# Reordering the first batch of a fused attention and mixer kernel: loads of pair 2, second mask, casts, second-layer weights, and a cleared mask table

## The chip, the cores and the metric

One core of one Trainium2 chip. The metric is the device time of one execution in microseconds (us), the median of several executions. The engines are named PE (matmul), ACT (scalar), DVE (vector), GpSimd (POOL in the profile) and SyncE (SP in the profile, which here only issues transfers).

## The reference, cut to what matters

Attention over 4 batches, 8 heads, 768 positions, head size 64, with a block mask (blocks of 32: neighbours, first and last blocks, three sampled blocks per row), then a mixer:

```python
scores = where(mask, q @ k.T / 8, -1e9);  attn = softmax(scores);  x = attn @ v
u  = x + (x.T @ U @ V).T                       # low rank, over positions
out = u + relu(u @ w_ch1) @ w_ch2              # 512 -> 2048 -> 512
```

The result is float32 of shape 4x768x512. The kernel works on pairs of heads: 16 pairs, 4 in each batch. Pair 0 to pair 3 are batch 0, the first batch.

## The kernel before: the parts that matter

In the first batch the mask is put into the scores by the matmul itself: the lower or upper 64 rows of `qa` and `ka` hold mask rows and one-hot rows. There are two sets of `qa` and `ka`, used by even and odd pairs; the mask rows of set 1 are a copy of those of set 0. The four queue heads at the start, with the table `small` first on ACT's queue:

```python
keep(nc.scalar.dma_start(out=small[0:NB], in_=small_dr.ap()))      # NB = 24 rows
keep(nc.sync.dma_start(out=qld[:, :, 0:TQ], in_=q0[:, :, 0:TQ]))
keep(nc.scalar.dma_start(out=kld[:, :, 0:TK], in_=k0[:, :, 0:TK])) # k's first piece
keep(nc.sync.dma_start(out=qld[:, :, TQ:T], in_=q0[:, :, TQ:T]))
keep(nc.scalar.dma_start(out=id16, in_=eye16_dr.ap()))
keep(nc.sync.dma_start(out=kld[:, :, TK:T], in_=k0[:, :, TK:T]))
...                                       # (cut)
vld = new_ld(0, "v")                      # v waits on purpose for k's first piece
keep(nc.gpsimd.tensor_copy(out=vld[:, 0, 0, 0:1], in_=kld[:, 0, 0, 0:1]))
keep(nc.sync.dma_start(out=vld, in_=src_of("v", 0)))
issue(1)                                  # pair 1's q, k, v on SyncE's queue
```

Every pair has nine units. A unit is: scores on PE, one exp of 128x1024 on ACT, values of the unit three back on PE, then what `at_unit` adds. Program order is kept on each engine:

```python
for i in range(HP):                       # HP = 4 pairs
    for u in range(NU):                   # NU = 9 units
        scores(i, u, ests[u])             # matmuls, then exp on ACT
        ...                               # (cut) values of an earlier unit
        at_unit(i, u)

def at_unit(i, u):
    if i == 0 and u == 0:                 # (cut to the part that is changed)
        for h in range(2):
            mask_rows("dve", h, pm2[:, 0, 0:QB], QA, S)
            nc.sync.dma_start(out=qa[1][h][mrows[h], :], in_=qa[0][h][mrows[h], :])
            hot_rows(nc.sync, 1, h, D)    # one-hot rows into ka[1]
        ...                               # V twice, U, then pair 2's q and k
        cast(1, "q"); cast(1, "k"); cast(1, "v")      # float32 to float16 on GpSimd
    ...
    if u == 6: cast(i + 2, "q"); cast(i + 2, "k")
    if u == 8: cast(i + 2, "v")
    for _ in range({0: 1, 5: 2, 6: 1, 7: 1}.get(u, 0)):
        if tails: tails.popleft()()       # mixer of the pair before: its xh and uh casts are on GpSimd
```

From the second batch on, scores, values and the two layers of the mixer are interleaved on PE by a fixed schedule.

The softmax here doesn't subtract the row's maximum and nothing guards it: scores larger than these inputs give would overflow.

## Time and profile before

| | before |
|---|---|
| median (3 runs at first; 283.31 to 283.8) | 283.8 us |
| span of the profiled run | 281.8 us |
| first exp starts | 7.26 us |
| first 37 exps (batch 0 and one more) end | 45.44 us |
| idle between these exps | 2.51 us |
| PE's unbroken mixer stream starts (22 matmuls `pt`) | 50.77 us |

Windows by stage of the kernel before. Columns: stretch, its length, busy time (and instructions) of PE, PE's weight loads, DVE, ACT, GpSimd, then PE's granted clock, the mean busy share of the 16 DMA engines, and GB/s.

```profile
52.00:60.00 8.00, 8.00 (x100) 4.34 (x98) 6.63 (x12) 7.43 (x12) 0.00 (x0) 1.00 2.65 125
...
80.00:120.00 40.00, 39.85 (x596) 23.63 (x594) 33.42 (x50) 29.49 (x32) 23.34 (x27) 1.00 1.27 124
```

From 52 us on PE is busy almost without a break (39.85 of each 40 us from 80 to 200 us, 19.58 of the 20 before that). A start that is earlier or later by some amount moves what is behind it by that amount (the mixer stream starts at 50.77 us here and at 51.98 in the changed kernel, and DVE's last addition ends 227.89 and 227.92 us later). So the first batch decides, and there ACT's exps are the longest work. The timeline of ACT, kernel before; columns are start, length, engine and line, operation, tiles and shapes, count, and in brackets the idle time before and what ended it.

```profile
4.66 0.40 ACT L362 CAST kst<-kld 128x256 f16<-128x256 f32 x1 [0.27 <-DMA kld<-in_k_dram]
...
7.26 6.90 ACT L494 ACTIVATE est<-psc 128x1024 f16<-128x1024 f32 x7 [0.54 <-PE psc L174]
14.49 4.69 ACT L494 ACTIVATE est<-psc 128x1024 f16<-128x1024 f32 x5 [0.33 <-PE psc L174]
19.47 3.97 ACT L494 ACTIVATE est<-psc 128x1024 f16<-128x1024 f32 x4 [0.29 <-PE psc L174]
23.95 2.94 ACT L494 ACTIVATE est<-psc 128x1024 f16<-128x1024 f32 x3 [0.51 <-PE psc L174]
28.26 17.18 ACT L494 ACTIVATE est<-psc 128x1024 f16<-128x1024 f32 x18 [1.38 <-PE psc L174]
46.28 1.94 ACT L494 ACTIVATE est<-psc 128x1024 f16<-128x1024 f32 x2 [0.84 <-PE psc L174]
```

Read it so: 18 exps in 17.18 us is ACT's own pace, 0.95 us each. Where a row ends and a new one begins, ACT had to wait for scores: 0.33, 0.29, 0.51 and 1.38 us. The last row is the step into the second batch, 0.84 us idle. The chain of waits of the kernel before, ahead of the largest gap (start, length, what):

```profile
15.62 6.63 DMA vld<-in_v_dram
...
25.07 0.83 POOL kst L248
25.91 0.45 POOL uh L655
26.35 0.47 POOL w1t L434
26.83 0.52 POOL uh L655
...
27.39 0.34 PE puT L707 x3
...
28.26 0.80 ACT est L494
```

The casts of `uh` (the mixer's float16 input for the transposes `puT`) stand on GpSimd behind pair 3's k cast, with a weight-load issue between them, and all this behind a late load of v; PE's transposes `puT` wait for uh, and the scores stand behind the transposes. SyncE's queue in the same kernel:

```profile
7.10 0.54 SPq L991 DMA_DIRECT2D qa<-qa  x1
...
8.38 0.53 SPq L991 DMA_DIRECT2D qa<-qa  x1
...
9.60 1.07 SPq L1000 DMA_DIRECT2D w2t<-in_moe_V_dram  x2
...
14.46 0.38 SPq L233 DMA_DIRECT2D qld<-in_q_dram  x1
```

Pair 2's q is issued at 14.46 us, behind the mask copies, V and U.

### The profile page before, as it was taken

Reading aid. Unit: us, or ns where it says so; the run is one execution under the profiler, and the core shown is the slowest. Engines: PE = TensorE matmul, PEld = TensorE weight load, DVE = VectorE, ACT = ScalarE, POOL = GpSimd, SP = SyncE. Lnnn points to the kernel's source line nnn. Section 1 sums busy time; section 2 is a strip of 40 time slices with the busy share of each in tenths; the row PEclk is TensorE's granted clock in tenths of the full one; section 3 lists DMA queues with packets and bytes.
Section 4 is the critical chain, followed back from the end, with each engine's and each line's share of the span. In section 5 each row is a group of like instructions: output and inputs, shape, how many; then the busy total and the mean of one; then the engine's idle time right before and its main releaser. Section 6 shows DMA issues by size and latency. Waiting matters only on the chain.

```text
span 281.8 us, 8050 instructions
## 1 busy us (share of the span) xinstructions
PE 272.5 (97%) x3497; PEld 162.3 (58%) x3497; DVE 175.1 (62%) x285; ACT 177.5 (63%) x199; POOL 100.5 (36%) x132
## 2 busy tenths in 40 slices
PE   8997998999999999999999999999999999999995
PEld 3565775456566564656665555657565544655443
DVE  6765767797888878765967767784979541000112
ACT  4997997696969847595876657596868101654000
POOL 2379857205356646361614545361102020000000
PEclk9999999999999999999999999999999999999999
DMA  5989999993979999997794999993100313000112
GB/s 173 268 240 333 238 247 187 155 117 25 95 75 112 155 122 148 139 131 83 49 123 28 142 100 134 167 111 55 30 2 2 102 22 128 31 1 2 74 74 77
DMA packets 85716, 31.71 MB, mean 112 GB/s; under 512 B 75304, under 2 KB 83312, under 8 KB 85680
## 3 DMA queue, kind: packets, MB, share of 16 engines
q0 software_dynamic: 49728, 10.10, 47.7%
q1 hardware_dynamic: 35464, 20.85, 35.0%
q8 instruction: 27, 0.44, 0.6%
q10 hardware_dynamic: 488, 0.24, 0.3%
q14 instruction: 9, 0.07, 0.1%
HBM read 27.90 MB, written 6.29 MB: 121 GB/s over the span
## 4 chain that ended last, share of the span: by engine, by line
PE 79%; DMA 6%; ACT 6%; POOL 3%; issue 2%; DVE 1%; SPq 1%; ACTq 0%; POOLq 0%; DVEq 0%
PE pt L174 29%; PE pch L174 28%; PE pav L174 10%; PE psc L174 8%; ACT est L494 6%; DMA vld<-in_v_dram 5%; PE pa L174 2%; DMA kld<-in_k_dram 1%; POOL xh L594 1%; PE ph L174 1%; POOL uh L655 1%; POOL vt L242 1%; POOL w1t L434 0%; SPq L233 0%; DVE xh L537 0%
## 5 line engine op out<-in xcount | busy, mean ns | idle before, releaser
L494 ACT ACTIVATE est<-psc 128x1024 f16<-128x1024 f32 x144 | 142.5, 1028 | 42.0 <-PE psc L174 40.4
L174 PE MATMUL pt<-uT,w1t 64*128 64x384 f16 (+1 forms) x896 | 94.6, 324 | 0.5 <-ACT est L494 0.4
L174 PE MATMUL pch<-w2t,tT 64*128 64x512 f16 (+3 forms) x688 | 93.3, 372 | 0.2
L515 DVE TENSOR_TENSOR est<-est,m 128x1024 f16<-128x1024 f16 x108 | 78.7, 745 | 17.2 <-ACT est L494 16.0
L174 PEld LDWEIGHTS <-w1t 64*128 64x128 f16 (+1 forms) x896 | 46.7, 94 | 36.5 <-PE pt L174 6.7
L174 PEld LDWEIGHTS <-tT 64*128 64x128 f16 (+1 forms) x688 | 37.7, 95 | 38.5 <-PE pch L174 1.4
L732 ACT ACTIVATE tT<-pt 128x768 f16<-128x768 f32 (+1 forms) x48 | 36.8, 776 | 33.7 <-PE pt L174 33.7
L174 PEld LDWEIGHTS <-est 128*128 128x128 f16 x1152 | 41.4, 97 | 10.9 <-issue 5.1
L174 PE MATMUL pav<-vt,est 128*128 128x65 f16 x1152 | 44.4, 193 | 0.1
L594 POOL CAST xh<-xs 128x768 f16<-128x768 f32 x12 | 11.5, 955 | 86.5 <-DVE xs L585 55.9
L787 DVE TENSOR_TENSOR of<-xf,pch 128x1024 f32<-128x1024 f32 (+3 forms) x16 | 15.3, 954 | 43.5 <-PE pch L174 43.4
L174 PE MATMUL psc<-qT,kT 64*128 64x512 f16 (+1 forms) x288 | 40.8, 323 | 0.0
L680 POOL CAST uh<-xf 128x768 f16<-128x768 f32 x12 | 13.0, 1087 | 25.2 <-issue 12.9
L174 PE MATMUL psc<-qa,ka 128*128 128x512 f16 (+1 forms) x96 | 21.5, 326 | 0.3
L734 DVE TENSOR_SCALAR tT<-pt 128x768 f16<-128x768 f32 (+1 forms) x20 | 18.2, 916 | 4.6 <-PE pt L174 4.5
L174 PEld LDWEIGHTS <-kT 64*128 64x128 f16 x288 | 14.4, 94 | 11.0 <-DVE xs L585 0.2
L262 POOL DMA_DIRECT2D qst<-in_q_dram x20 | 16.3, 821 | 0.1
L262 POOL DMA_DIRECT2D vt<-in_v_dram x20 | 16.3, 822 | 0.0
L262 POOL DMA_DIRECT2D kst<-in_k_dram x20 | 16.3, 821 | 0.0
L583 DVE RECIPROCAL rcp<-pav 128x12 f32<-128x12 f32 x12 | 2.8, 233 | 16.0 <-PE pav L174 16.0
L585 DVE TENSOR_TENSOR xs<-pav,rcp 128x768 f32<-128x768 f32 x12 | 11.5, 958 | 1.2
L671 DVE TENSOR_TENSOR xf<-xs,ph 128x768 f32<-128x768 f32 x12 | 11.4, 950 | 1.3 <-PE ph L174 1.1
(68 smaller groups left out, 134.8 us busy)
## 6 DMA issues: line engine op xcount, KB each, us to landing
out_dram<-of SPq DMA_DIRECT2D x9, 512.0 KB, 3.7
vld<-in_v_dram SPq DMA_DIRECT2D x6, 384.0 KB, 8.0
w1t<-in_moe_w_ch_dram POOLq DMA_DIRECT2D x4, 512.0 KB, 10.7
w2t<-in_moe_w_ch_dram POOLq DMA_DIRECT2D x4, 512.0 KB, 18.4
qld<-in_q_dram SPq DMA_DIRECT2D x5, 384.0 KB, 6.2
kld<-in_k_dram SPq DMA_DIRECT2D x5, 384.0 KB, 7.2
qst<-in_q_dram POOLq DMA_DIRECT2D x20, 96.0 KB, 3.9
kst<-in_k_dram POOLq DMA_DIRECT2D x20, 96.0 KB, 4.8
```

Source lines behind the costliest of these rows:

```text
L174: ins = nc.tensor.matmul(out, lhsT, rhs, start=start, stop=stop, skip_group_check=loose)
L242: nc.gpsimd.tensor_copy(out=vts[b % 2][:, 2 * hp : 2 * hp + 2, :, 0:D], in_=ld)
L262: keep(nc.gpsimd.dma_start(out=o[:, h], in_=src_of(nm, i)[:, h]))
L494: keep(nc.scalar.activation(out=est, in_=psc, func=AF.Exp, scale=0.125))
L515: keep(nc.vector.tensor_tensor(out=o, in0=o, in1=m, op=ALU.mult))
L585: nc.vector.tensor_tensor(out=xs.rearrange("p (c j) (h d) -> p c (j h) d", c=2, h=2), in0=pv[:, :, :, 0:D], in1=rcp[:, :, :, None].broadca ...
L594: keep(nc.gpsimd.tensor_copy(out=xh, in_=xs))
L671: nc.vector.tensor_tensor(out=u.rearrange("p (c j) n -> p c j n", c=2), in0=xs.rearrange("p (c j) n -> p c j n", c=2), in1=ph[:, :, 0:HS]. ...
L680: keep(nc.gpsimd.tensor_copy(out=uh, in_=u))
L732: keep(nc.scalar.activation(out=o, in_=i, func=AF.Relu))
L734: keep(nc.vector.tensor_scalar_max(out=o, in0=i, scalar1=0.0))
L787: nc.vector.tensor_add(out=of, in0=xfs[b][:, sc : sc + nsc, n0:n1], in1=pch)
```

## The change

The intent, as I read it from the diff: get pair 2's loads out early, by taking the second mask's four transfers from SyncE's queue to GpSimd's; put the casts that PE waits for ahead of those for loads to come; load the second layer's weights only in the second batch; and run the mask matmuls on all 128 rows, for which the rest of the table has to be cleared first. (The third pair is pair 2 here, as pairs count from 0.)

```diff
+    keep(nc.gpsimd.memset(small, 0.0))
     keep(nc.scalar.dma_start(out=small[0:NB], in_=small_dr.ap()))
...
-            cbd[0:NB].rearrange("z a c -> z (a c)"),      # mask matmuls
-            small[0:NB, a:e],
+            cbd.rearrange("z a c -> z (a c)"),
+            small[:, a:e],
...
-    for vt in vts:                                        # moved to the start
-        keep(nc.gpsimd.memset(vt[:, :, :, D : D + 1], 1.0))
+    for h in range(2):
+        hot_rows(nc.gpsimd, 1, h, D)
     cast(0, "v")
...
-            ((1, 3), (1, 5), (1, 7), (2, 0), (2, 3), (2, 5), (2, 7), (3, 0))
+            ((1, 3), (1, 4), (2, 3), (2, 4), (HP, 0), (HP, 2), (HP, 4), (HP, 6))
...                                                        # at_unit(0, 0)
-                    keep(nc.sync.dma_start(out=qa[1][h][mrows[h], :], in_=qa[0][h][mrows[h], :]))
-                    hot_rows(nc.sync, 1, h, D)
-                V twice, U, issue(2, "qk")
+                issue(2, "q"), U, issue(2, "k"), V twice
                 cast(1, "q")
+                for h in range(2):
+                    keep(nc.gpsimd.dma_start(out=qa[1][h][mrows[h], :], in_=qa[0][h][mrows[h], :]))
                 cast(1, "k")
...
             if u == 6:
+                cast(2, "q")
                 cast_U()
-                cast(2, "q")
...
-        at = u - 2 if i == 1 else u - 1                   # turns of the next pair
-        if at in range(4): ...
-        if u == 6: cast(i + 2, "q"), cast(i + 2, "k")
-        if u == 8: cast(i + 2, "v")
+        if u in (1, 2, 3, 4): ...
         ... tails ...
+        if u == 7: cast(i + 2, "q")
+        if u == 8: cast(i + 2, "k")
+        if u == 0 and i > 1: cast(i + 1, "v")
```

(Cut: the hook that issues the weight loads in the second batch, and the v cast of pair 5 there. Lines of several statements are drawn together.)

More of the change, by code (lines that the diff above doesn't have):

```diff
@@ L314 @@
     keep(nc.scalar.activation(out=dummy, in_=zeros[:, 0:1], func=AF.Exp))
+    for vt in vts:
+        keep(nc.gpsimd.memset(vt[:, :, :, D : D + 1], 1.0))
     vld = new_ld(0, "v")
@@ L989, in at_unit @@
                     mask_rows("dve", h, pm2[:, 0, 0:QB], QA, S)
-                    keep(
-                        nc.sync.dma_start(
-                            out=qa[1][h][mrows[h], :], in_=qa[0][h][mrows[h], :]
-                        )
-                    )
-                    hot_rows(nc.sync, 1, h, D)
                 for nm, o, pt, t in (("q", qa[0], pq, TQ), ("k", ka[0], pk, TK)):
@@ L998, in at_unit @@
                         half_copy(nc.vector.tensor_copy, o, h, pt, t, T)
-                for h in range(2):
-                    keep(nc.sync.dma_start(out=mvld[h * R : h * R + R], in_=moe_V))
+                issue(2, "q")
                 keep(
@@ L1005, in at_unit @@
                 )
-                issue(2, "qk")
+                issue(2, "k")
+                for h in range(2):
+                    keep(nc.sync.dma_start(out=mvld[h * R : h * R + R], in_=moe_V))
                 cast(1, "q")
+                for h in range(2):
+                    keep(
+                        nc.gpsimd.dma_start(
+                            out=qa[1][h][mrows[h], :], in_=qa[0][h][mrows[h], :]
+                        )
+                    )
                 cast(1, "k")
@@ L1034, in at_unit @@
             WLOADS[i, u]()
-        at = u - 2 if i == 1 else u - 1
-        if at in range(4):
-            turn_part(i + 1, "qk"[at // 2], at % 2)
-        if u == 6:
-            cast(i + 2, "q")
-            cast(i + 2, "k")
-        if u == 8:
-            cast(i + 2, "v")
+        if u in (1, 2, 3, 4):
+            turn_part(i + 1, "qk"[(u - 1) // 2], (u - 1) % 2)
         for _ in range({0: 1, 5: 2, 6: 1, 7: 1}.get(u, 0)):
@@ L1045, in at_unit @@
                 tails.popleft()()
+        if u == 7:
+            cast(i + 2, "q")
+        if u == 8:
+            cast(i + 2, "k")
+        if u == 0 and i > 1:
+            cast(i + 1, "v")
     for i in range(HP):
@@ L1069, in unit_sides @@
             turn_dma(i + 1, "k")
+        if (i, u) in WLOADS:
+            WLOADS[i, u]()
         if u in (3, 5, 7):
@@ L1104 @@
             flush_value()
+            cast(HP + 1, "v")
         if gi == 1:
```

## The prediction

> **What bounds the kernel now.** From about 48 us to the end PE is busy without a break (windows by stage: 39.85 of each 40 us), clock 1.00. The change adds nothing to that part (same instruction counts on PE, ACT, DVE; order differs only in the first batch). Time can only come from the first 48 us, the attention of batch 0, where the chain of waits runs over ACT. ACT does 36 exps of 128x1024 there, about 0.95 us each in an unbroken run (18 in 17.18 us), from 7.26 us: never starved, they would end at 41.6. In the timeline they end about 44.5: idle before exps 0.33 (14.49), 0.29 (19.47), 0.51 (23.95), 1.38 us (28.26), 2.5 us in all. PE transposes stand in program order before the scores and wait for the GpSimd casts of pair 1's k (landed 12.6), pair 2's q (issued only at 14.46, landed 17.8) and, at 28.26, for uh casts queued behind pair 3's q and k casts and weight-load issues. Then the transition: pair 2's uh cast waits behind pair 5's k cast, which waits 2.8 us for a load that took 17.4 us under the weight loads; PE's puT waits till 45.27, ACT idles 0.84.
>
> **What the change does.**
> - Second mask's four copies (96 KB, 7.3 to 7.6 us to landing) leave SyncE's queue, so pair 2's q and k issue near 7.5 to 9 us. DMA share was only about 0.4 at 14 to 16 us; that slack is filled. Removes the 0.29 us gap. [...] The 0.33 us gap stays.
> - xh and uh casts come before the next pair's q and k casts: removes most of 1.38 and 0.51 us, and about 1 us of the transition.
> - Four second-layer weight loads (512 KB, 18.4 us to landing) go to 43 to 50 us; pair 5's loads land earlier. Weights are first used at 81.6 us: in time. GpSimd's issues of pair 6's v must wait for two of them; GpSimd is idle 51 to 66.3, enough.
> - Clearing the small table on GpSimd (128x816) precedes its load, first on ACT's queue; k's first piece follows. Estimate 0.6 us (cast of 128x768: 0.83; two 128x48 memsets: 0.53): first exp 7.26 to about 7.8.
>
> **Sum (estimates).** Gaps -1.8, transition -0.9, late start +0.5, new waits at pair 1 (the second set's masks issue only after pair 1's q cast) or in the second batch 0 to 0.5: about -2.1 us.
>
> Predicted 281.7 us, 80% range 279.5 to 283.7. Chances: faster by over 2% 0.04, within 2% 0.93, slower 0.03.
>
> **What would show it.** First exp near 7.8 us. Pair 2's q issued before 9 us, cast near 16. ACT idle between the 36 exps under 1 us; 36th ends near 43. PE continuous from about 46. Second-layer weights landed before 65, no pch wait near 80. Windows after 60 us shifted by about 2 us only.
>
> **What would make it wrong.** The clear costing over 1 us; pair 1's transposes starved because the mask copies slow its loads (gap over 1 us near 12 to 16 us); pair 1's scores waiting for the second mask; GpSimd blocked on weight loads past 66, delaying xh and pair 6's loads; or later stages absorbing the gain.

## The result, and the profile after

The changed kernel took 283.9 us (4 runs, 283.79 to 284.18) against 283.8 us before (4 runs, 283.31 to 284.05). The ratio is 1.0007, 95% interval 0.999 to 1.0025: the same. A ratio is the mean time of one kernel's runs over that of the other's in the same rounds, so it is not quite the ratio of the medians quoted.

The same views as before. ACT's timeline of the changed kernel:

```profile
7.19 0.40 ACT L365 CAST kst<-kld 128x256 f16<-128x256 f32 x1 [1.94 <-DMA kld<-in_k_dram]
...
10.95 8.73 ACT L497 ACTIVATE est<-psc 128x1024 f16<-128x1024 f32 x9 [1.80 <-PE psc L174]
20.69 26.60 ACT L497 ACTIVATE est<-psc 128x1024 f16<-128x1024 f32 x28 [1.01 <-PE psc L174]
47.50 1.94 ACT L497 ACTIVATE est<-psc 128x1024 f16<-128x1024 f32 x2 [0.21 <-PE psc L174]
```

Two things are opposite to each other. The gaps of before are gone: 28 exps run in 26.60 us, again 0.95 us each, and the step into the second batch idles 0.21 instead of 0.84 us. But the first exp starts at 10.95 instead of 7.26 us, and there is a new gap of 1.01 us before the tenth exp, which is pair 1's first. The chain of waits of the changed kernel's start shows both:

```profile
0.74 0.78 POOL w1t L306
...
2.14 5.03 DMA kld<-in_k_dram
...
7.22 0.19 POOL vld L321
...
7.85 3.87 DMA qld<-in_q_dram
...
11.78 0.23 POOL qst L248
...
12.55 0.51 POOL qa L1008
13.05 7.18 DMA qa<-qa
...
20.28 0.39 PE psc L174
```

The clear of the table on GpSimd is the first piece of work. ACT's queue waits for it, then issues the table, and k's first piece at 2.14 us (1.35 us before); this lands after 5.03 us (3.29 us before). Further down the mask copies qa to qa are issued behind pair 1's q cast and land 7.18 us later.

The accounting, all from the two profiles:

| stretch | before | after | difference |
|---|---|---|---|
| to the first exp | 7.26 | 10.95 | +3.69 |
| first exp to the end of the 37th | 38.18 | 36.34 | -1.84 |
| from there to PE's unbroken stream | 5.33 | 4.69 | -0.64 |
| from there to the end of DVE's last addition | 227.89 | 227.92 | +0.03 |
| from there to the end of the span | 3.14 | 2.50 | -0.64 |
| span | 281.8 | 282.4 | +0.6 |

Some 2.5 us were gained in the first batch and the step out of it, and 3.7 us were lost before the first exp. The second batch and what follows are neutral, as the windows of the changed kernel show (up to 240 us PE is busy to the hundredth as before):

```profile
52.00:60.00 8.00, 8.00 (x96) 4.22 (x97) 6.86 (x12) 6.21 (x11) 3.98 (x5) 1.00 1.43 189
...
80.00:120.00 40.00, 39.85 (x603) 23.75 (x601) 32.92 (x48) 28.65 (x30) 22.64 (x27) 1.00 1.22 122
```

Then there is PE's clock. Windows of the start, changed kernel:

```profile
4.00:5.00 1.00, 0.36 (x2) 0.00 (x0) 0.24 (x2) 1.00 (x1) 0.00 (x0) 1.00 0.77 170
5.00:6.00 1.00, 0.55 (x3) 0.31 (x4) 0.82 (x4) 0.24 (x2) 0.00 (x0) 1.00 0.93 294
6.00:7.00 1.00, 0.39 (x3) 0.10 (x1) 0.58 (x1) 0.00 (x0) 0.00 (x0) 1.00 0.17 49
7.00:8.00 1.00, 0.45 (x5) 0.44 (x5) 0.00 (x0) 0.81 (x2) 0.78 (x3) 0.71 0.00 0
8.00:9.00 1.00, 1.00 (x6) 0.44 (x4) 0.79 (x3) 0.67 (x3) 1.00 (x3) 0.50 0.43 69
9.00:10.00 1.00, 1.00 (x4) 0.44 (x3) 0.81 (x3) 0.15 (x1) 0.47 (x1) 0.50 0.99 369
10.00:11.00 1.00, 1.00 (x5) 0.31 (x4) 0.00 (x0) 0.05 (x1) 0.41 (x1) 0.58 1.20 344
```

PE stood idle for more than half of 4 to 7 us (it waited 1.09 us for the table's mask, then 1.17 us for the identity matrix), and then its clock was at half for 0.58 + 1 + 1 + 0.84 = 3.42 us (worked out from the clock column: a mean of 0.71 is 0.58 us at half).

The packed traces of the two kernels show more than this one stretch. They hold the clock as records, and up to the last one the lengths of these are whole steps of 3.41 us (changed: 3.413 us at full clock from 4.01 us, 3.413 at half, then 273.066 at full, which is 80 steps; before: 276.48 at full from 4.65 us, which is 81). Worked out over all 162 of these windows at full clock in the two profiles: each of the three in which PE was busy for 1.29 us or less is followed by half clock, and none of the 159 in which it was busy for 2.37 us or more. (Two of the three lie at the end of the kernels, where PE runs out of work: 0.62 us busy in before and none in changed. The third is this one, 4.01 to 7.42 us with 1.29 us busy. One of a_noclear_qaearly below is like it.) All four runs of the changed kernel have a mean granted clock of 0.994, as the profiled one has with its one such window. One caution: before a profile's first record, or where it has none, the clock column says 1.00 even while PE runs at half rate (in a_noclear below it says 1.00 from 6 to 10 us, where four warming matmuls took 1.91 us). The eight warming matmuls (on dummy data, to keep PE busy) with which all kernels but a_warm start take 3.2 to 3.6 us, where four later ones take 1.03 us at full rate. So at the start the length of a matmul decides, not the column.

### The profile page after: what moved, and what is told of

Same layout as the page of the kernel before. It is cut to its first block, busy times and chain, and to the rows that moved or that the text cites. A ratio compares the mean times of both kernels' runs of the same rounds, so it can differ in the third digit from the quotient of the medians.

```text
span 282.4 us, 8047 instructions
## 1 busy us (share of the span) xinstructions
PE 273.4 (97%) x3497; PEld 163.0 (58%) x3497; DVE 174.9 (62%) x285; ACT 177.1 (63%) x199; POOL 103.2 (37%) x137
## 4 chain that ended last, share of the span: by engine, by line
PE 79%; ACT 9%; DMA 6%; POOL 2%; issue 2%; DVE 1%; ACTq 0%; SPq 0%; DVEq 0%; POOLq 0%
PE pt L174 29%; PE pch L174 28%; PE pav L174 10%; ACT est L497 9%; PE psc L174 8%; DMA qa<-qa 3%; DMA kld<-in_k_dram 2%; PE pa L174 2%; DMA qld<-in_q_dram 1%; POOL xh L597 1%; PE ph L174 1%; DVE xh L540 0%; DVE xs L588 0%; POOL w1t L306 0%; PE puT L702 0%
## 5 line engine op out<-in xcount | busy, mean ns | idle before, releaser
L174 PE MATMUL psc<-qa,ka 128*128 128x512 f16 (+1 forms) x96 | 22.1, 331 | 1.2 <-DMA qa<-qa 0.9
```

The costliest lines, as they stand in the source:

```text
L174: ins = nc.tensor.matmul(out, lhsT, rhs, start=start, stop=stop, skip_group_check=loose)
```

## The experiments

Theory: the clear holds back ACT's queue and with it k; PE idles and loses its clock; the mask copies hold pair 1; the rest of the change gains what was predicted. Rivals are named in each expectation. Sixteen kernels ran, each in 5 rounds against the kernel before on the same chip (before's median 283.4 to 283.9 us there). All gave the right result. Runs of one kernel differ: in several kernels they fall into two groups some 2 us apart (c_copy: five at 280.0 to 280.6 and one at 282.8), so a difference of medians under about 1 us is weak evidence. Times after the ratio are from the one profiled run of each.

| kernel | median us (range) | ratio to before | first exp | idle between the first 37 exps | 37th exp ends |
|---|---|---|---|---|---|
| before | 283.8 | | 7.26 | 2.51 | 45.44 |
| changed | 283.9 (283.79 to 284.18) | 1.0007 | 10.95 | 1.01 | 47.29 |
| a_noclear | 282.94 (281.99 to 285.59) | 0.9981 | 9.53 | 0.98 | 45.81 |
| b_clear | 286.42 (284.5 to 286.69) | 1.0073 | 9.27 | 4.17 | 49.10 |
| a_clear_aside | 283.21 (282.37 to 284.83) | 0.9984 | 9.53 | 0.56 | 45.51 |
| a_warm | 284.26 (284.11 to 287.75) | 1.0038 | 9.32 | 2.52 | 47.28 |
| a_qaearly | 282.94 (282.75 to 283.44) | 0.9985 | 10.35 | 0.17 | 45.86 |
| a_noclear_qaearly | 282.56 (281.47 to 283.8) | 0.9971 | 7.60 | 3.43 | 46.65 |
| a_padded_qaearly | 282.62 (281.33 to 285.39) | 0.9984 | 7.99 | 2.08 | 45.52 |
| a_kfirst_qaearly | 282.11 (281.44 to 283.61) | 0.9955 | 9.75 | 0 | 45.15 |
| c_copy | 280.21 (279.97 to 282.83) | 0.9903 | 8.49 | 0 | 43.74 |
| c_copy_w2early | 280.09 (279.72 to 280.26) | 0.9882 | 7.63 | 0 | 42.87 |
| c_copy_oldcasts | 281.21 (280.71 to 283.13) | 0.9946 | 7.91 | 0.51 | 43.91 |
| c_oldloads | 281.79 (281.31 to 282.88) | 0.9947 | 8.49 | 0 | 43.73 |
| a_copy | 282.54 (281.52 to 282.86) | 0.9949 | 10.13 | 0 | 45.37 |
| c_copy_last3 | 281.34 (280.02 to 282.67) | 0.9912 | 8.17 | 0.15 | 43.43 |
| c_copy_last0 | 281.71 (280.61 to 282.36) | 0.992 | 8.30 | 0 | 43.55 |
| c_copy_w2early_24 | 281.73 (279.77 to 282.05) | 0.9915 | 9.40 | 0 | 44.63 |

### a_noclear: the changed kernel without the clear

```diff
-    keep(nc.gpsimd.memset(small, 0.0))
-            cbd.rearrange(...), small[:, a:e]            # back to 24 rows
+            cbd[0:NB].rearrange(...), small[0:NB, a:e]
```

> The changed kernel without the clear of the small table and with the mask matmuls back on 24 rows. Theory (the clear holds back ACT's queue, k's first piece lands late, PE idles and its clock is halved; the rest of the change gains about 2.5 us): first exp at 7.2 to 7.8 us as before instead of 10.95, granted clock 1.00 from 8 to 16 us, time about 280.5 to 281.5 us. Rival 1 (the late start is due to the moved copies and loads, not the clear): first exp stays near 10.9 and time near 283.9. Rival 2 (the first batch is not on the critical path): first exp early, time unchanged.

k's cast started at 4.56 us (4.66 before the change). The first exp, at 9.53 us, missed the expected 7.2 to 7.8, and the time missed it too. PE ran at half rate in this profile: its four warming matmuls behind the first transposes took 1.91 us, against 1.03 us in the kernel before. PE had not idled here, it was busy without a break from 1 to 11 us, and the first clock record at full rate is at 9.94 us. So my theory had too little in it: the clear explains k, but the clock can come late without it.

### b_clear: the kernel before with the clear alone

```diff
+    keep(nc.gpsimd.memset(small, 0.0))                  # ahead of the table's load
-            cbd[0:NB].rearrange(...), small[0:NB, a:e]
+            cbd.rearrange(...), small[:, a:e]
```

> The kernel before with the clear and the 128-row mask matmuls alone. Theory: first exp near 10.9 us, clock below 1 between 7 and 11 us, time 286 to 287.5 us (3 us over before, a little less where the gaps of the first batch shrink because loads have more time). Rival 1 (not the clear): within 0.5 us of before.

```profile
7.08 0.41 ACT L363 CAST kst<-kld 128x256 f16<-128x256 f32 x1 [1.83 <-DMA kld<-in_k_dram]
...
9.27 6.90 ACT L495 ACTIVATE est<-psc 128x1024 f16<-128x1024 f32 x7 [0.54 <-PE psc L174]
```

k's cast at 7.08 us, first exp at 9.27 us with PE at full rate: the clear with its wait (and the 128-row mask matmuls) costs 2.01 us before the first exp, without any help from the clock. The expected 10.9 us and the lower clock did not come: PE's window from 5.73 us had 2.33 us of work, and the clock stayed up. The median rose by 2.5 us over before. This falls in the expected range, and the first rival falls.

### a_clear_aside: the same clear where nothing waits for it

```diff
-    keep(nc.gpsimd.memset(small, 0.0))
+    keep(nc.gpsimd.memset(<816 columns of w2t, not loaded until later>, 0.0))
```

(and 24-row mask matmuls.)

> The changed kernel with 24-row mask matmuls, and the clear done with the same size on a piece of the weight tile for which no early load waits. Theory (the cost is the wait of ACT's queue for the clear, not GpSimd's work): like a_noclear, first exp 7.2 to 7.8, 280.5 to 281.5 us. Rival (GpSimd's memset slows DVE or DMA by itself): first exp above 9 us.

k's cast at 4.66 us, first exp at 9.53 us as in a_noclear. GpSimd's work itself did not delay k; the wait for it did. The expected first exp was missed, for the same reason as in a_noclear (four warming matmuls in 1.91 us).

### a_warm: more matmuls to keep PE busy while it waits

```diff
-    warm_pe(8)
+    warm_pe(10)
...
-    warm_pe(1)
+    warm_pe(4)
```

> The changed kernel with two more warming matmuls before the mask matmuls and three more after them, to fill PE's idle 4.4 to 5.5 and 6.4 to 7.6 us. Theory (part of the late start, about 1.2 us, is PE at half its granted clock from 8 to 10.6 us after idling): clock 1.00 throughout, k's first piece still lands near 7.2, first exp near 9.8 to 10 us, time about 1 us under the changed kernel (282.7 to 283.2). Rival (the clock is not tied to PE's idleness): clock still 0.5 near 8 to 10 us and no gain.

ACT's timeline of a_warm:

```profile
7.06 0.41 ACT L365 CAST kst<-kld 128x256 f16<-128x256 f32 x1 [1.82 <-DMA kld<-in_k_dram]
...
9.32 6.90 ACT L497 ACTIVATE est<-psc 128x1024 f16<-128x1024 f32 x7 [0.54 <-PE psc L174]
16.48 1.94 ACT L497 ACTIVATE est<-psc 128x1024 f16<-128x1024 f32 x2 [0.27 <-PE psc L174]
20.68 26.60 ACT L497 ACTIVATE est<-psc 128x1024 f16<-128x1024 f32 x28 [2.25 <-PE psc L174]
```

The start did come 1.63 us earlier (9.32), yet the tenth exp starts at 20.68, where it started at 20.69. All that was won was waited off: 2.25 us ahead of pair 1. So a second hold, which does not move with the first exp, fixes the tenth exp, and it is the one seen in the chain of waits: pair 1's q cast, the issue of the copies behind it, and their 7 us. It is not independent of the clear. v's load waits on purpose for k's first piece, and pair 1's loads stand behind v's, so in the changed kernel pair 1's q was issued at 7.85 us, against 5.33 before. Where k was in time and the copies stood as in the changed kernel, the tenth exp started at 19.20 us (a_noclear) and 18.90 (a_clear_aside). That the changed kernel's clock fell for want of work on PE agrees with this run (full rate, by four warming matmuls in 1.03 us, after filling the idle time), but this run alone does not prove it: b_clear stayed at full rate with the idle time not filled.

### a_qaearly: mask copies issued ahead of pair 1's q cast

```diff
                 issue(2, "k"), V twice
-                cast(1, "q")
                 copies qa[0] -> qa[1] on GpSimd's queue
+                cast(1, "q")
                 cast(1, "k")
```

> The changed kernel with the two copies of the mask (qa to qa) issued on GpSimd ahead of pair 1's q cast instead of behind it. Theory (after the late start there is a second hold: these copies are issued at 12.6 us because they stand behind a cast that waits for pair 1's q, and land 7 us later, so pair 1's first exp cannot begin before about 20.7 us whatever the first exp does): issue near 10 to 11 us, the gap of 1.0 us before the 10th exp gone or under 0.4 us, time 0.6 to 1 us under the changed kernel, 282.9 to 283.3 us. Rival (the copies land when they land because DMA is full): gap as before, time 283.9.

Issue at 11.24 us (a little later than expected), landing 6.7 to 7.0 us later, gap 0.17 us, and 282.94 us, as expected.

### a_noclear_qaearly: both undone

> Both undone: no clear, 24-row mask matmuls, copies ahead of the cast. Theory: no gap before the 10th exp, 36th exp ends 0.7 us or more before a_noclear's (45.0), time 281.5 to 282.5 us; runs in which PE stays on half clock to 10 us (24-row mask matmuls) about 1.5 us longer than those in which it is warm by 5 us. Rival (the two holds are not additive, DMA sets the 10th exp): as a_noclear, 282.9 us.

Here PE was at full rate and the first exp at 7.60 us. But the copies, issued at 9.33 us, were waited for still longer. PE's timeline, a_noclear_qaearly:

```profile
17.36 0.38 PE L174 MATMUL psc<-qa,ka 128*128 128x512 f16 x1 [1.70 <-DMA qa<-qa]
18.44 0.38 PE L174 MATMUL psc<-qa,ka 128*128 128x512 f16 x1 [0.70 <-DMA qa<-qa]
```

The scores of pair 1 wait 1.70 us for one copy and 0.70 us for the other: they landed at about 17.3 and 18.4 us, 8 us after their issue. My expectation "no gap" fell and its rival was right: an earlier place on GpSimd's queue does not bring them in time. Beside them ran the loads of pairs 1 and 2 that the change pulled forward, and the mean busy share of the DMA engines was 1.02 to 1.10 from 9 to 18.4 us in the windows of this run. That these loads made the copies late is my guess and not shown: no run has the copies without such loads beside them. Another issuer did not shorten them: on GpSimd's queue the copies took 7.9 to 8.6 us, on SyncE's, in the kernel before, 7.6. The wait also cost PE its clock: in the window from 15.57 to 18.98 us PE was busy for 1.01 us, and from 18.98 to 22.40 us it ran at half clock; the further gaps of 0.59 and 0.32 us fall in this stretch and just behind it. The profile is of one of the slower runs (283.54 us): the three with a mean clock of 0.993 to 0.994 took 282.8 to 283.8 us, the three at 0.999 to 1.0 took 281.5 to 282.3, so the median of 282.56 mixes the two.

### a_padded_qaearly: a padded table in place of the clear

```diff
-    small_np = np.concatenate([...])                    # 24 rows
+    small_np = np.zeros((P, S + 2 * NB)); small_np[:NB] = np.concatenate([...])
-    out=small[0:NB], in_=small_dr.ap()
+    out=small, in_=small_dr.ap()
```

(and the copies ahead of the cast.)

> No clear: the table comes from memory already padded with zeros to 128 rows (209 KB instead of 38 KB), mask matmuls on 128 rows, copies ahead of the cast. Theory ([...]only the wait for the clear was bad): clock warm by 5 to 7 us, first exp 7.5 to 8.5 us, 10th exp with a gap below 0.4 us, time 280.5 to 282 us. Rival (the longer table load delays k as much as the clear did): first exp over 9 us at full clock.

First exp at 7.99 us as expected; but gaps of 1.10 and 0.98 us, where pair 1's transposes waited for k's cast and its scores for the mask copies, against an expected 0.4. The copies landed 8.1 to 8.3 us after their issue; that the 209 KB table had a part in this is not shown. The time, 282.62 us, is over the expected range.

### a_kfirst_qaearly: k's first piece ahead of the table

```diff
-    table load, then k's first piece                    # ACT's queue
+    k's first piece, then clear (GpSimd) and table load
```

(and the copies ahead of the cast.)

> The changed kernel with k's first piece issued on ACT's queue ahead of the table (the clear still precedes the table), copies ahead of the cast. Theory (k's landing was late because its issue stood behind the table's wait): k lands near 4 us as in before, the table near 4.7 us, so the masks set the start: first exp about 8 us, time 281 to 282.3 us. Rival (k lands at 7.2 us for another reason, such as the load of DMA): first exp near 10.9 us.

k's cast at 4.42 us with the clear still in the program: it was the place in the queue that made k late. First exp at 9.75 us, not the expected 8, with PE at half rate until 9.1 us in this profile; no gap after it, since it came so late. 282.11 us, within the expected range.

### c_copy: k first, and GpSimd copies the mask itself

The copy's source and target are the same rows of two tiles, and GpSimd can write them itself: in this run its two copies of 64x768 took 1.70 us together, and the result was right.

```diff
                 cast(1, "q")
-                copies qa[0] -> qa[1] by nc.gpsimd.dma_start
                 cast(1, "k")
+                for h in range(2):
+                    keep(nc.gpsimd.tensor_copy(out=qa[1][h][mrows[h], :], in_=qa[0][h][mrows[h], :]))
```

(and k's first piece ahead of the table.)

> The changed kernel with k's first piece issued ahead of the table (as in a_kfirst_qaearly), and the second mask's rows copied by GpSimd itself (64x768, estimate 0.6 to 0.9 us each from its cast of 128x768 at 0.83) after pair 1's k cast instead of by DMA. Theory (late start and mask copies were the two holds; the copies land 7 to 8 us after issue wherever they are issued[...]): no wait for qa at pair 1's first scores, one unbroken run of 36 exps even when the first exp is early, time 281 to 282 us, below a_kfirst_qaearly when PE warms early. Rival (the loads themselves now set the pace): a gap of over 0.5 us at pair 1, as in a_noclear_qaearly.

GpSimd's and ACT's timelines, c_copy:

```profile
11.50 1.70 POOL L1009 COPY qa<-qa 64x768 f16<-64x768 f16 x2
13.16 0.82 POOL L242 CAST vt<-vld 128x768 f16<-128x768 f32 x1
...
8.49 35.25 ACT L497 ACTIVATE est<-psc 128x1024 f16<-128x1024 f32 x37 [0.54 <-PE psc L174]
43.95 1.94 ACT L497 ACTIVATE est<-psc 128x1024 f16<-128x1024 f32 x2 [0.22 <-PE psc L174]
```

Both copies took 1.70 us together, and 37 exps run in 35.25 us without a gap. The time is 280.21 us, ratio 0.9903 (0.9873 to 0.9933): 1% under before, and below the expected range. Both holds were the cause, and taking both away gives 3.6 us by the medians, more than the predicted 2.1. (PE was also at full rate when the first scores ran in this profile, which the edit does not ensure; it was not in a_kfirst_qaearly. ACT waited 0.54 us for its first scores here, 1.36 us there.)

### c_copy_w2early, c_copy_oldcasts, c_oldloads: one part of the change undone in each

```diff
# c_copy_w2early: weight loads at the places of before
-            ((1, 3), (1, 4), (2, 3), (2, 4), (HP, 0), (HP, 2), (HP, 4), (HP, 6))
+            ((1, 3), (1, 5), (1, 7), (2, 0), (2, 3), (2, 5), (2, 7), (3, 0))
# c_copy_oldcasts: casts at u == 6 and u == 8, pair 1's turns one unit later, U's cast ahead of pair 2's q
# c_oldloads: SyncE's queue as before (mask copies and one-hot rows by DMA, V, U, then pair 2), no copy by GpSimd
```

> c_copy with the weight loads at their places of before (second-layer weights in the first batch). Theory (moving them frees DMA for pair 4's and 5's loads and GpSimd's queue): pair 5's q and k casts wait again for their loads near 40 us and stand ahead of no uh cast now, so PE's loss is small: time 0 to 0.7 us above c_copy; first 27 exps unbroken. Rival (the weight move is what closed the gaps): exps broken at pairs 2 and 3, 1 us or more above c_copy.

No gaps, 280.09 us (4 runs): with the other parts of the change in place, moving the weight loads was worth nothing in time.

> c_copy with the casts and transposes in the order of before (next pair's q and k casts ahead of uh, U ahead of pair 2's q). Theory (the 0.51 and 1.38 us gaps were GpSimd order): gaps of 0.5 to 1.4 us near the ends of pairs 1 and 2 come back, time 1 to 2 us above c_copy. Rival (the gaps came from late loads): no gaps, time as c_copy.

The 0.51 us gap came back, at the same exp (the 17th); the 1.38 us gap did not. 1.0 us above c_copy by the medians, of which the profiles show 0.75 us within the 37 exps. So the cast order is worth the 0.51 us gap by itself; the 1.38 us gap stayed away with the old casts. Something else that c_copy_oldcasts kept of the change (the places of the weight loads or of pair 2's loads, for instance) was enough to remove it; which, was not run. The runs fall into groups here too (280.7 to 280.8 three times, 281.6 to 283.1 three times).

> c_copy with SyncE's queue in the order of before: the mask copies and one-hot rows by DMA ahead of V, U and pair 2's q and k. Theory (the load order alone cost the wait for qa and gained only the 0.29 us gap): pair 2's q issued near 14 us, with transposes a unit earlier PE waits for its cast: a gap of 0.5 to 1.5 us near unit 1 of pair 1, no gap for qa; time 0.3 to 1.5 us above c_copy. Rival (early loads of pair 2 buy nothing): time as c_copy.

The expected gap did not appear: 37 exps in 35.24 us. With the new cast order the early loads of pair 2 gain nothing in the first batch (37th exp ends at 43.73 us, against 43.74 in c_copy). The span is nevertheless 0.7 us longer, all of it after DVE's last addition (the medians differ by 1.6 us; what the other 0.9 us are, the profiles do not show, so it is open whether the early loads gain anything). That opened the question of the end.

### c_copy_last3, c_copy_last0: the end of the kernel

In all profiles so far with the changed order on SyncE's queue, 2.48 to 2.51 us pass from DVE's last addition to the end of the span; in the three with the old order (before, b_clear, c_oldloads) 3.09 to 3.19 us. (The tables' spans are rounded to 0.1 us.) The old order has four more transfers on that queue, so the last store signals another one of the eight semaphores that the transfers take in turn: number 3, and number 7 in the new order.

```diff
+    for d in range(4):                                  # 1 in c_copy_last0
+        keep(nc.sync.dma_start(out=spare[d : d + 1], in_=oh_dr.ap()[d : d + 1, 0:D]))
```

> c_copy with four tiny transfers (128 bytes each) on SyncE's queue near 48 us, where it is idle, so that the last store uses the same completion semaphore (number 3 of 0 to 7) as in the kernel before instead of number 7. Theory (the end depends on which semaphore is last): from the end of DVE's last addition to the end of the span 3.1 us as in before, not 2.5; time 0.6 us above c_copy. Rival (the end is shorter through the changed loads of the first batch): 2.5 us, time as c_copy.

> The same with one tiny transfer: the last store on semaphore number 0. Theory (each semaphore checked after the last one costs about 0.16 us, so four cost 0.6 and seven 1.1): end 3.6 us after DVE's last addition, time 1.1 us above c_copy. Rival: 2.5 us.

The end took 2.73 us (last on number 3) and 2.91 us (number 0), against an expected 3.1 and 3.6, and 2.48 us in c_copy. So there is a dependence of about 0.06 us for each semaphore, and it is too small: in the traces SyncE's last waits follow each other at 0.06 us, one for each semaphore behind that of the last store. It accounts for 0.25 of some 0.7 us. In before and c_oldloads the other 0.44 us lie at GpSimd's last drain instruction, which ends 0.56 us after the barrier ahead of it, against 0.12 in c_copy; b_clear does not fit this, and the reason stays open. The medians, 281.34 and 281.71 us, are 1.1 and 1.5 us above c_copy, which the end does not explain: the runs fall into two groups, and the profiled ones are of the faster group (280.59 and 280.87 us, c_copy's 280.58).

### a_copy: the changed kernel with only the copies taken to GpSimd

```diff
                 cast(1, "q")
-                copies by nc.gpsimd.dma_start
                 cast(1, "k")
+                copies by nc.gpsimd.tensor_copy
```

> The changed kernel with the clear still ahead of the table and k, and only the mask copies done by GpSimd. Theory: first exp at 9.3 us (PE warm) to 10.9 us (PE at half clock for a window), then 36 exps unbroken; time 1 to 2 us above c_copy, 281 to 282.5 us, and 1.5 to 2.5 us below the changed kernel. Rival (the clear cost little by itself): within 0.5 us of c_copy.

282.54 us, at the edge of the expected range: 1.4 us below the changed kernel, from taking the mask's hold away. What is left to c_copy, 2.3 us by the medians and 1.7 us by the spans, is the order of clear, table and k, with PE at half rate to about 9.5 us in a_copy's profile and not in c_copy's.

### c_copy_w2early_24: no clear, mask matmuls on 24 rows

```diff
# c_copy_w2early, and:
-    keep(nc.gpsimd.memset(small, 0.0))
-            cbd.rearrange(...), small[:, a:e]
+            cbd[0:NB].rearrange(...), small[0:NB, a:e]
```

> c_copy_w2early without the clear and with 24-row mask matmuls, k's piece still issued first. Theory (128 rows buy nothing but a chance to keep PE's clock up; without the clear the table lands 0.5 us earlier): first exp 7.3 to 7.8 when PE is warm by 5 us, 9 to 9.6 when not; best runs 279.3 to 279.7 us, wider spread than c_copy_w2early, median 279.5 to 281. Rival (128 rows are needed for the clock): median over 281 us.

PE's timelines of the mask matmuls and what follows. First c_copy_w2early_24:

```profile
4.61 1.24 PE L174 MATMUL pm<-w1t,cbd 24*128 24x512 f16 x3
...
6.82 1.91 PE L174 MATMUL warm<-m 128*128 128x512 f16 x4
8.53 0.83 PE L174 MATMUL psc<-qa,ka 128*128 128x512 f16 x2
```

and c_copy_w2early, with 128 rows:

```profile
5.04 0.71 PE L174 MATMUL pm<-w1t,cbd 128*128 128x512 f16 x3 [0.45 <-DVE cbd L353]
...
6.14 1.03 PE L174 MATMUL warm<-m 128*128 128x512 f16 x4
7.00 0.59 PE L174 MATMUL psc<-qa,ka 128*128 128x512 f16 x2
```

With 24 rows the three mask matmuls took 1.24 us and the four warming ones 1.91 us, half the rate of 0.71 and 1.03. The median of 281.73 us is above the expected range, where the rival had put it. The times fall into two groups: 279.77 us once, 281.49 to 282.05 us five times. With 128 rows c_copy_w2early has all four runs at 279.7 to 280.3 us, and c_copy five of six at 280.0 to 280.6 (and one at 282.8). Of five kernels with 24 rows that were profiled, counting before, three were at half rate when the first scores ran (ACT waited 1.58 to 1.80 us for them, against 0.54 in the other two). One window speaks for the rows: in a_noclear PE was busy for all of 3.11 to 6.53 us, 1.2 us of it on 24 rows and 0.4 us in transposes, and its rate did not rise (the four warming matmuls from 6.73 us took 1.91 us). So the clear may well have a purpose, to let PE's clock rise in time. But four of the thirteen profiles with 128 rows (changed, a_qaearly, a_kfirst_qaearly, a_copy) were at half rate there as well (waits of 1.36 to 1.80 us, against 0.54 in the other nine), c_copy_last3 has two groups of times too (280.0 to 280.6 three times, 282.1 to 282.7 three times) with 128 rows, and only a profile shows the start, as the runs' mean clock leaves it out (1.0 in a_noclear's profiled run). It is possible, not shown.

## Why the prediction was wrong, point by point

The prediction was 281.7 us, 279.5 to 283.7; the result was 283.9. It is just outside the range. The class "within 2%" was right.

- **What bounds the kernel, and where time could come from: right.** From the stream's start to DVE's last addition the two kernels differ by 0.03 us in 228. Nothing was lost in the second batch, though GpSimd waited there for the moved weight loads: this line of the changed kernel's groups shows 3.5 us of it in all, and GpSimd was idle anyway until its next cast at 67.5 us.

```profile
L262 POOL DMA_DIRECT2D vt<-in_v_dram x20 | 16.3, 820 | 3.5 <-DMA w2t<-in_moe_w_ch_dram 3.5
```

- **Gaps -1.8 and transition -0.9: right in kind.** All four old gaps (2.51 us) went; with the new one the 37 exps took 1.84 us less. The transition gave 0.64. The reasons were only half right: c_copy_oldcasts ties the 0.51 us gap to the order of casts, but c_oldloads shows that pair 2's early loads, which the prediction held to be worth the 0.29 us gap, show no gain within the 37 exps once the casts are reordered, and c_copy_w2early shows the same of the weight loads. What removed the 1.38 us gap stays open.
- **"Late start +0.5": the step that failed.** It measured +3.69 us. The estimate for the clear itself was 0.6 us and it took 0.78, and k's issue moved by 0.79. I took the delay of the issue for the delay of the landing. In its place: k then stood behind q's pieces and landed 5.03 us after issue, not 3.29, so its cast came 2.53 us later (a_kfirst_qaearly: back at 4.42 us with the clear still there). That it was the company of q's pieces which made the landing longer is argued, not shown. From k's cast to the first exp another 1.16 us were lost, with PE at half clock for 3.42 us after a window in which it was busy for 1.29 of 3.41 us. At full clock b_clear has +2.01 us in all. I had listed "the clear costing over 1 us" among what could go wrong, without weighing it.
- **"New waits at pair 1 ... 0 to 0.5": the second term that was mis-sized.** The visible gap was 1.01 us, but this is what remained after the start had come late by 3.7 us. With the start 1.63 us earlier it was 2.25 us (a_warm), and 2.52 us with the start at 7.60 us (a_noclear_qaearly). The two holds overlap: with the start at 7.60 us the 37th exp still ended at 46.65 us in a_noclear_qaearly, later than the 45.44 of before, so the mask copies alone could undo the gain of the first batch. And part of the copies' lateness came from the clear too, through pair 1's late q. Without the copies' wait, a_copy was 1.4 us faster.
- **Not predicted:** the end of the kernel came 0.64 us sooner. Only part of that is explained.

## What to carry to other kernels

A delay on a queue was not passed on one to one here: a transfer that was issued 0.79 us later landed 2.53 us later, and PE, which had 1.29 us of work in a window of 3.41 us while it waited, was at half clock for the next 3.41 us. When a start is moved, look for the next thing with a fixed time behind it: here an earlier start alone gained nothing (a_warm), an earlier issue of the copies did not bring them in time (a_noclear_qaearly), and only both together, with the copies made by an engine instead of by DMA, brought 283.8 us to 280.2. And undo each part of a bundle: of the parts of this change the clear held the start back, the mask copies held pair 1 back, the cast order was worth about 0.5 to 1 us, the moved weights showed no gain of their own, and the early loads none in the first batch, though the kernel without them was 1.6 us slower for reasons that are only in part known.
